# Closing block of a one-core decode kernel: SyncE and ScalarE each await their own store, GpSimd clears its semaphore ranges while the stores fly, SyncE takes the engines' semaphores back

## The chip, the cores and the metric

The kernel runs on one core of a Trainium2 chip (trn2). The time is the device time of one execution, in microseconds. It is longer than the span of the profile, which runs from the start of the first recorded instruction of the kernel to the end of its last one: what the runtime puts ahead of the kernel and behind it has no instruction records in the profile.

## The reference

One token's row `x` (576 values) goes through an attention with a long cache (32 query heads, 16 key and value heads, of 32768 positions the last 4096) and through a dense layer with a gelu, and a gate mixes the two. Everything is bfloat16.

```python
W = min(4096, max(256, Sk // 4))                       # 4096
q = (x @ wq).reshape(B, Sq, Hq, Dh).transpose(0, 2, 1, 3)
k = jnp.repeat(k_cache[:, :, Sk - W:, :], 2, axis=1)   # v the same way
p = softmax(einsum("bhqd,bhkd->bhqk", q, k) * Dh ** -0.5)
a = einsum("bhqk,bhkd->bhqd", p, v).transpose(0, 2, 1, 3).reshape(B, Sq, Hq * Dh) @ wo
b = gelu(x @ w1 + b1) @ w2 + b2
g = sigmoid((x * gate_w).sum(-1, keepdims=True))
out = g * a + (1 - g) * b                              # one row of 576
```

## The kernel before, in words

Nearly all of the work is reading 53.6 MB from HBM: `w1`, `wq`, four loads of the keys, four of the values, `wo` and `w2`, all issued by SyncE's queue in this order, each as soon as its buffer is free. `w2` comes last, in pieces, the last two of 288 and 144 KB. TensorE multiplies each piece as it lands. The last eight columns of `w2` go through `y_late` (line 379), which writes into `y_ps` and `yb_ps`. Then ScalarE turns 192 columns of the result into `out_rows` (line 829) and VectorE the other 96 (line 830), and the two halves of the output row, 576 bytes each, are stored by two DMAs: one issued by ScalarE (line 834), the other by SyncE (line 835).

What follows is the closing block. The program's framework puts a block behind every kernel, in which all engines meet and GpSimd sets the kernel's semaphores back to zero, so that the next execution finds them so. The function `store_ends_program`, called when the program is finalized, replaces that block's list of instructions by a list of its own. In the lines of the profile all of this stands under line 861. These are the words of the function and what they stand for:

- `drain`, `arrive` and `leave` are SyncE's three instructions of the framework's block: the wait for everything, the step that tells the others that SyncE has come, and the wait for the release.
- A *drain* of another engine is an instruction that ends when the engine's work is done.
- S96 is the framework's gather semaphore, which each engine raises by one when it comes; S97 is the release semaphore.
- S99 is GpSimd's own semaphore, S105 VectorE's, S106 ScalarE's, S108 TensorE's; S101 to S104, S107 and S109 are those of loads. S100 is that of SyncE's store (value awaited: 64), S110 that of ScalarE's store (48).
- `lanes` are the semaphores that GpSimd leaves out of its clears because somebody else takes their value back. A taken semaphore is awaited and lowered by the awaited value in one instruction.
- `reset` and `clear` are the pair of instructions by which GpSimd clears a range of semaphores: a drain marked as a reset, and an `EVENT_SEMAPHORE_RANGE_CLEAR`.

The closing block before consists of these instructions, engine by engine:

- SyncE (3): raise S96; await S100 and take it back; await S110 and take it back.
- ScalarE, TensorE, VectorE (1 each): drain, then raise S96.
- GpSimd (10): four instructions that await eight semaphores in pairs (loads, S105, S106); a drain that awaits S99; await S96 at 4 and lower it by 4; then two pairs of reset and clear, for S99 alone and for S101 to S109.

So GpSimd clears only after SyncE, ScalarE, TensorE and VectorE have all come, and SyncE is the engine that waits for the two stores.

Of the kernel before, what the change touches and what calls it, by code (L numbers as in the profile page):

```python
# [18 lines left out]
def kernel(  # L19
# [95 lines left out]
    def store_ends_program(nc):  # L115
        body, end = nc.main_func.blocks[1], nc.main_func.blocks[2]
        sp, pool = mybir.EngineType.SP, mybir.EngineType.Pool
        store = [
            i
            for i in body.instructions  # L120
            if i.engine == sp and type(i).__name__ == "InstDMACopy"
        ][-1]
        act = mybir.EngineType.Activation
        store2 = [
            i
            for i in body.instructions
            if i.engine == act and type(i).__name__ == "InstDMACopy"
        ][-1]
        lanes = sorted(i.sync_info.on_update[0].id for i in (store2, store))
        names = [i.name for i in end.instructions if i.engine == sp]  # L130
        names += [i.name for i in end.instructions if i.engine == act][1:]
        drain, arrive, leave = [i for i in end.instructions if i.engine == sp][:3]
        waits = list(drain.sync_info.on_wait)
        mine = [next(w for w in waits if w.id == lane) for lane in lanes]
        waits = [w for w in waits if w.id not in lanes]
        kept = [
            copy.replace(
                leave,
                name=names.pop(),
                sync_info=mybir.SyncInfo(on_wait=[], on_update=arrive.sync_info.on_update),  # L140
            )
        ]
        for w, name in zip(mine, names):
            taken = mybir.SyncUpdate(
                sync_type="semaphore",
                id=w.id,
                ant_name=w.ant_name,
                update_mode="sem-sub-imm",
                update_value=w.wait_value,
                update_reg=None,  # L150
            )
            kept.append(
                copy.replace(
                    leave,
                    name=name,
                    sync_info=mybir.SyncInfo(on_wait=[w], on_update=[taken]),
                )
            )
        for engine in (
            mybir.EngineType.Activation,  # L160
            mybir.EngineType.PE,
            mybir.EngineType.DVE,
        ):
            kept.append(next(i for i in end.instructions if i.engine == engine))
        ours = [i for i in end.instructions if i.engine == pool]
        others = mybir.SyncInfo(on_wait=waits, on_update=[])
        kept += [copy.replace(ours[0], sync_info=others), ours[1]]
        reset, clear = ours[3:5]
        lo, hi = reset.reset_range_start, reset.reset_range_stop
        edges = [lo - 1, *lanes, hi]  # L170
        spans = [(a + 1, b) for a, b in zip(edges, edges[1:]) if a + 1 < b]
        fresh = [reset.name, clear.name, *[i.name for i in ours[5:7]], *names[len(mine) :]]
        assert len(fresh) >= 2 * len(spans)
        for n, (a, b) in enumerate(spans):
            raw = list(clear.instr)
            assert raw[13:15] == [lo, hi - 1]
            raw[13:15] = [a, b - 1]
            words = dict(clear.ant_dict, range_first=a, range_last=b - 1)
            kept.append(
                copy.replace(reset, name=fresh[2 * n], reset_range_start=a, reset_range_stop=b)  # L180
            )
            kept.append(copy.replace(clear, name=fresh[2 * n + 1], instr=raw, ant_dict=words))
        end.instructions = kept

    nc.at_finalize(store_ends_program)

    const = ctx.enter_context(tc.tile_pool(name="const", bufs=1))
# [34 lines left out]
    for base, pattern, keep in (  # L222
# [6 lines left out]
        n = 1  # L229
# [193 lines left out]
    for c0, src, q in ((0, h_s[0], 2), (1024, h_s[1], 2), (2048, h_m, 4)):  # L423
        n = 1024 if q == 2 else 256
# [92 lines left out]
    issued = {}  # L517
# [348 lines left out]
```

## Time and profile before

| what | value |
|---|---|
| median of 3 runs | 131.51 us (131.38 to 131.53) |
| profiled execution, device time | 131.67 us |
| its span | 130.17 us (130.2 on the page), so 1.50 us lie outside it |
| share of the span in which the chain that ended last waited for DMA | 86% |
| granted TensorE clock, mean | 0.869 |
| HBM read | 53.62 MB, 412 GB/s over the span |

The two profiled numbers belong together: the span holds the kernel's own instructions, closing block included, and the remaining 1.50 us are the runtime's. The trace also records every change of a semaphore, and those go on behind the span, to 131.754 us. The closing block is too short for the page's forty slices (3.25 us each); these are its records, in us from the span's start:

| engine | instruction | start | took, ns |
|---|---|---|---|
| TensorE | drain | 128.149 | 335 |
| VectorE | drain | 128.489 | 283 |
| SyncE | issue of its store | 128.793 | 277 |
| ScalarE | issue of its store | 128.801 | 248 |
| GpSimd | fourth paired wait (S109, S106) | 128.810 | 43 |
| GpSimd | drain, S99 | 128.897 | 41 |
| ScalarE | drain | 129.089 | 240 |
| SyncE | raise S96 | 129.118 | 17 |
| GpSimd | await S96 at 4 | 129.362 | 17 |
| GpSimd | reset, clear of S99 | 129.442, 129.531 | 60, 48 |
| GpSimd | reset, clear of S101 to S109 | 129.608, 129.708 | 70, 88 |
| SyncE | await and take S100 | 130.079 | 17 |
| SyncE | await and take S110 | 130.153 | 17 |

The instructions that wait have the start at which their wait was over. The landing of ScalarE's store is recorded at 129.888, that of SyncE's at 130.063.

### The profile page before, as it was taken

The page shows a single profiled execution, that of the slowest core. Times are in us where ns is not written, and L with a number is a line of the kernel's source. Part 1 is how long each engine was busy: PE and PEld are TensorE (multiplying, and loading weights), DVE is VectorE, ACT ScalarE, POOL GpSimd, SP SyncE. Part 2 cuts the span into 40 slices and gives each one's busy share as a digit, 9 for nine tenths or more (in the row PEclk, how much of TensorE's full clock was granted, in tenths as well). Part 3 has the DMA queues.
Part 4 walks back from the last instruction along what each step waited for, and adds up shares of the span by engine and source line. Part 5 has one row for each costly group of instructions (what it writes and reads, how often), then busy time and mean ns, then how long its engine had stood idle before and what let it go on. Part 6 is the DMA issues. An engine that isn't in the chain of part 4 may idle for free.

```text
span 130.2 us, 1168 instructions
## 1 busy us (share of the span) xinstructions
PE 81.5 (63%) x558; PEld 26.0 (20%) x416; DVE 61.1 (47%) x51; ACT 11.4 (9%) x27; POOL 10.0 (8%) x32
## 2 busy tenths in 40 slices
PE   0003999597106995949949955981075064799994
PEld 0003111310100221201212211331021020426552
DVE  0030003416199659999999995639205005100001
ACT  3032100210300000030003003030000000000000
POOL 7019700010000000000000000000100000000000
PEclk9999999999755799985999999999658757756999
DMA  7999999799899999999999999989989999999970
GB/s 255 398 437 432 476 419 487 342 483 453 383 453 463 398 423 463 433 393 463 433 393 473 423 393 473 453 357 483 435 385 463 451 417 428 417 414 416 398 319 22
DMA packets 2507, 53.70 MB, mean 413 GB/s; under 512 B 287, under 2 KB 420, under 8 KB 710
## 3 DMA queue, kind: packets, MB, share of 16 engines
q1 hardware_dynamic: 2490, 53.61, 96.4%
q8 instruction: 4, 0.07, 0.2%
q10 hardware_dynamic: 12, 0.01, 0.0%
q14 instruction: 1, 0.01, 0.0%
HBM read 53.62 MB, written 0.00 MB: 412 GB/s over the span
## 4 chain that ended last, share of the span: by engine, by line
DMA 86%; DVE 8%; PE 3%; SPq 1%; issue 0%; ACT 0%; DVEq 0%
DMA k_t<-in_A_k_cache_dram 31%; DMA w_t<-in_B_w_dram 29%; DMA v_t<-in_A_v_cache_dram 22%; DVE kt L543 7%; DMA rows<-in_A_x_dram 4%; PE s_ps L654 1%; DVE m L581 1%; PE y_ps L379 1%; SPq L748 0%; SPq L744 0%; SPq L750 0%; PE yb_ps L379 0%; ACT out_rows L829 0%; DVE mr L584 0%; DVEq L543 0%
## 5 line engine op out<-in xcount | busy, mean ns | idle before, releaser
L565 PE MATMUL s_ps<-kt,qz_flat 128*128 128x512 bf16 x128 | 32.5, 410 | 15.4 <-DVE kt L543 8.6
L543 DVE STREAM_TRANSPOSE kt<-k_t 128x4096 f32<-128x4096 f32 x8 | 35.3, 4433 | 5.2 <-DMA k_t<-in_A_k_cache_dram 5.2
L654 PE MATMUL s_ps<-v_t,pt 128*32 128x512 bf16 x96 | 9.1, 547 | 8.9 <-DMA v_t<-in_A_v_cache_dram 8.8
L565 PEld LDWEIGHTS <-qz_flat 128*128 128x128 bf16 x64 | 6.8, 107 | 38.5 <-issue 38.3
L668 DVE TENSOR_TENSOR own<-s_ps,is 128x512 f32<-128x512 f32 x3 | 2.1, 685 | 15.3 <-PE s_ps L654 15.3
L602 ACT ACTIVATE p_t<-s_ps,negm 128x1024 bf16<-128x1024 f32 x4 | 4.5, 1114 | 47.5 <-DVE negm L598 47.5
L400 PE MATMUL s_ps<-w_t,x 128*32 128x512 bf16 x36 | 6.5, 622 | 1.6 <-DVE x L328 1.6
L320 PE MATMUL xs_ps<-ident,rows 1*128 1x1 bf16 x9 | 0.6, 189 | 10.7 <-POOL ident masks.py:199 10.7
L821 DVE COPY y_part<-y_ps 33x96 f32<-33x96 f32 x1 | 0.2, 250 | 14.7 <-PE y_ps L365 14.7
L654 PEld LDWEIGHTS <-pt 128*32 128x32 bf16 x128 | 3.7, 118 | 14.3 <-DMA v_t<-in_A_v_cache_dram 9.2
L425 DVE STREAM_TRANSPOSE turned<-s_ps 128x1024 f32<-128x1024 f32 x2 | 2.5, 1250 | 8.3 <-PE s_ps L400 8.3
L614 DVE STREAM_TRANSPOSE pt<-p_t 128x1024 bf16<-128x1024 bf16 x4 | 4.9, 1225 | 2.7 <-ACT p_t L602 2.7
L365 PE MATMUL y_ps<-wo_t,ov 128*1 128x288 bf16 x62 | 5.7, 359 | 0.3 <-DMA wo_t<-in_A_wo_dram 0.3
L400 PE MATMUL s_ps<-wq_t,x 128*32 128x512 bf16 x36 | 4.9, 620 | 0.9 <-DMA wq_t<-in_A_wq_dram 0.9
L581 DVE TENSOR_REDUCE m<-s_ps 128x1 f32<-128x1024 f32 x4 | 4.8, 1196 | 1.1 <-PE s_ps L565 1.1
L689 PE MATMUL mt_ps<-is,summed 128*128 128x8 f32 x8 | 1.6, 266 | 5.9 <-DVE summed L678 5.9
L705 POOL TENSOR_TENSOR ls<-is,sums 128x32 f32<-128x32 f32 x1 | 0.2, 238 | 60.2 <-ACT p_t L602 60.2
L334 DVE CUSTOM_DVE_ANT_0 rows<-rows 1x576 bf16<-1x576 bf16 x1 | 0.7, 746 | 8.2 <-DMA rows<-in_gate_w_dram 8.2
L678 DVE TENSOR_REDUCE summed<-own 128x128 f32<-128x512 f32 x4 | 4.2, 1041 | 0.1
L365 PEld LDWEIGHTS <-ov 128*1 128x1 bf16 x62 | 3.3, 103 | 3.9 <-issue 1.8
L806 PE MATMUL s_ps<-p_t,ones 128*128 128x512 f32 (+1 forms) x6 | 3.9, 739 | 0.0
L365 PE MATMUL y_ps<-w_t,gt 128*1 128x288 bf16 x56 | 3.8, 286 | 0.0
(87 smaller groups left out, 57.2 us busy)
## 6 DMA issues: line engine op xcount, KB each, us to landing
k_t<-in_A_k_cache_dram SPq DMA_DIRECT2D x4, 4096.0 KB, 33.2
v_t<-in_A_v_cache_dram SPq DMA_DIRECT2D x4, 4096.0 KB, 15.6
wq_t<-in_A_wq_dram SPq DMA_DIRECT2D x1, 4608.0 KB
wo_t<-in_A_wo_dram SPq DMA_DIRECT2D x1, 4464.0 KB, 28.2
w_t<-in_B_w_dram SPq DMA_DIRECT2D x1, 2880.0 KB, 14.3
w_t<-in_B_w_dram SPq DMA_DIRECT2D x1, 2592.0 KB
w_t<-in_B_w_dram SPq DMA_DIRECT2D x1, 2304.0 KB, 8.2
w_t<-in_B_w_dram SPq DMA_DIRECT2D x1, 1440.0 KB
```

Source lines behind the costliest of these rows:

```text
L365: last = nc.tensor.matmul(y_ps[32 * s : 32 * s + wide, :], lhsT=vec, rhs=row[:, DH * s : DH * s + DH], start=start, stop=stop, skip_group_ ...
L400: nc.tensor.matmul(last[n][32 * g : 32 * g + 32], lhsT=vec, rhs=part(n), start=start and g0 == 0, stop=g0 + 4 + g >= len(pieces), skip_gro ...
L425: nc.vector.transpose(out=turned[:, c0 : c0 + n], in_=src[:].rearrange("p (q l j) -> p q j l", q=q, l=32),)
L543: lambda: nc.vector.transpose(out=kt[g, f][:].bitcast(FP32), in_=keys.rearrange("p c d -> p (c d)").bitcast(FP32),),
L565: last = nc.tensor.matmul(s_ps[g][:, u * 512 : (u + 1) * 512].rearrange("p (c k) -> p c k", k=32), lhsT=qz(g, j, 2 * f + half), rhs=kv[:, ...
L581: queue("dve", lambda: nc.vector.reduce_max(out=m1[:], in_=s_ps[g][:], axis=AX.X))
L602: nc.scalar.activation(out=p_t[:].rearrange("p c k -> p (c k)"), in_=s_ps[g][:], func=ACT.Exp, bias=negm[:, 0:1], scale=SCALE, accum_out=s ...
L614: lambda: nc.vector.transpose(out=pt[:, g, :, :].rearrange("p c q -> p (c q)"), in_=p_t[:].rearrange("p c k -> p (c k)"),),
L654: last = nc.tensor.matmul(acc[g][32 * (c % 4) : 32 * (c % 4) + 32, :], lhsT=pt[:, g, c, :], rhs=v_t[g][:, c:NCK:32, :], start=(c < 4), sto ...
L668: lambda: nc.vector.tensor_tensor(out=own[:], in0=acc[g].rearrange("p (c d) -> p c d", c=4), in1=same_c.rearrange("p (c o) -> p c o", o=1) ...
L678: lambda: nc.vector.tensor_reduce(out=summed[g][:], in_=own[:].rearrange("p c d -> p d c"), axis=AX.X, op=ALU.add,),
L806: lambda: nc.tensor.matmul(spare[:, 0:item], lhsT=ones[:], rhs=p_t[:].rearrange("p c k -> p (c k)").bitcast(FP32)[:, 0:item], start=True, ...
```

## The change

The closing block's list is made differently. SyncE no longer raises S96; it awaits S97 (raised by ScalarE's drain, which in exchange no longer raises S96), takes it back, then awaits and takes S105, S106 and S108, and last its own store's S100. ScalarE gets a second instruction behind its drain, which awaits and takes its own store's S110. TensorE's and VectorE's drains raise S96 as before, without the (always fulfilled) wait for S97 at zero. GpSimd awaits the six loads in three pairs and S99 in its drain, no longer S105 and S106; it awaits S96 at 2 in place of 4; and as five semaphores are now left out, it clears four ranges in place of two: S99, S101 to S104, S107, S109.

| engine | instructions in the closing block before | after |
|---|---|---|
| SyncE | 3 | 5 |
| ScalarE | 1 | 2 |
| TensorE, VectorE | 1 each | 1 each |
| GpSimd | 10 | 13 |

```diff
-        lanes = sorted(i.sync_info.on_update[0].id for i in (store2, store))
+        sem, sem2 = (i.sync_info.on_update[0] for i in (store, store2))
...
-        mine = [next(w for w in waits if w.id == lane) for lane in lanes]
-        waits = [w for w in waits if w.id not in lanes]
-        kept = [
+        engines = [n for n in waits if n.startswith(("DVE", "Activation"))]
+        mine = [waits.pop(n) for n in engines]
+        mine.append(
             copy.replace(
-                leave,
-                name=names.pop(),
-                sync_info=mybir.SyncInfo(on_wait=[], on_update=arrive.sync_info.on_update),
+                mine[0],
+                id=pe[0].id,
+                ant_name=pe[0].ant_name,
+                wait_value=sum(u.update_value for u in pe),
             )
-        ]
+        )
+        mine.append(waits.pop(sem.ant_name))
+        last = waits.pop(sem2.ant_name)
+        lanes = sorted(w.id for w in [*mine, last])
+        release = copy.replace(leave.sync_info.on_update[0])
+        issued = copy.replace(release, update_mode="sem-inc")
+        kept = [copy.replace(leave, name=names.pop())]
...
-            kept.append(next(i for i in end.instructions if i.engine == engine))
+            done = next(i for i in end.instructions if i.engine == engine)
+            told = [issued] if engine == act else done.sync_info.on_update
+            kept.append(
+                copy.replace(done, sync_info=mybir.SyncInfo(on_wait=[], on_update=told))
+            )
+        kept.append(
+            copy.replace(
+                [i for i in end.instructions if i.engine == act][1],
+                sync_info=mybir.SyncInfo(
+                    on_wait=[last],
...
         ours = [i for i in end.instructions if i.engine == pool]
-        others = mybir.SyncInfo(on_wait=waits, on_update=[])
-        kept += [copy.replace(ours[0], sync_info=others), ours[1]]
+        others = mybir.SyncInfo(on_wait=list(waits.values()), on_update=[])
+        came = ours[1].sync_info
+        two = mybir.SyncInfo(
+            on_wait=[copy.replace(came.on_wait[0], wait_value=2)],
+            on_update=[copy.replace(came.on_update[0], update_value=2)],
+        )
+        kept += [copy.replace(ours[0], sync_info=others), copy.replace(ours[1], sync_info=two)]
```

## The prediction

> **What bounds the kernel now.** I read the page's chain first, to see whether the closing block is on it.
>
> ```profile
> DMA 86%; DVE 8%; PE 3%; SPq 1%; issue 0%; ACT 0%; DVEq 0%
> ```
>
> The kernel is bound by its loads; nothing in the change touches them, so all it can move lies behind the last of them. The timeline of the end shows where that is.
>
> ```profile
> 128.23 0.21 PE L379 MATMUL yb_ps<-w_t,gt 128*1 128x96 bf16 x2
> 128.44 0.31 ACT L829 CAST out_rows<-y_ps 33x192 bf16<-33x192 f32 x1 [16.13 <-PE yb_ps L379]
> 128.47 0.25 DVE L830 TENSOR_TENSOR out_rows<-yb_ps,y_part 33x96 bf16<-33x96 f32 x1 [1.43 <-PE yb_ps L379]
> 128.79 0.28 SPq L835 DMA_DIRECT2D out_dram<-out_rows  x1
> 128.80 0.25 ACTq L834 DMA_DIRECT2D out_dram<-out_rows  x1
> ```
>
> Both stores are issued at 128.8. Behind them comes line 861, the closing block, asked for by line (columns: engine, instruction, how many, shortest/median/longest in ns, first and last start).
>
> ```profile
> L861 POOLq DRAIN  x3: 41/60/70, 128.9 to 129.6; - x3
> L861 SPq EVENT_SEMAPHORE  x3: 17/17/17, 129.1 to 130.2; - x3
> L861 POOLq EVENT_SEMAPHORE_RANGE_CLEAR  x2: 48/68/88, 129.5 to 129.7; - x2
> L861 ACTq DRAIN  x1: 240/240/240, 129.1 to 129.1; - x1
> ```
>
> By these rows GpSimd is done at 129.8 and SyncE, waiting for the stores, ends the span at 130.170. That suggests that only SyncE counts. The semaphore records behind the span say otherwise. The device time (131.67) reaches 1.50 us past the span, and in that stretch one semaphore of the runtime, S2, steps nine times, at 128.729, 129.483, 130.324, 130.368, 130.392 and then 130.489, 130.528, 130.562, 130.608; some 0.8 us later it steps nine times more with nothing left to wait for: 131.397, .431, .469, .513, .536, .635, .673, .708, .754. It is a chain through the five engines and back, with free hops of 34, 38, 44 and 23 ns, then 99, 38, 35 and 46. Between the two passes some 250 semaphores are set back. In the first pass the hops into the fourth and fifth engine were 44 and 24 ns, the free ones: those two were ready already, and **whoever is third came last**.
>
> Who is third? The first step (128.729) can only be TensorE's: no other engine was through. The second (129.483) follows ScalarE's drain (129.089 + 0.240 = 129.329) by 0.154. For the rest I compare with the release at the program's start: S97 is raised at 0.705 and lowered by SyncE 34 ns later, by ScalarE after 45, by VectorE after 58; GpSimd answers the gather (0.578) after 49. Less 11 to 14 ns, these are the free hops: 23 (fifth, SyncE), 34 (second, ScalarE), 38 (third, GpSimd), 44 (fourth, VectorE). So I take the third to be **GpSimd**, whose last clear ended at 129.708 + 0.088 = 129.796, and which stepped 0.528 later. SyncE, done at 130.170, was ready before its turn at 130.368.
>
> **The change part by part.**
>
> *GpSimd's start.* Before, its wait for S96 at 4 ended at 129.362, after ScalarE's drain (its raise at 129.338). After, S96 needs TensorE (raised 128.498) and VectorE (128.783); with the same 24 ns it ends at 128.807. The paired waits ahead of it are over by then: the last load's semaphore came at 128.106, and S105 and S106 are no longer awaited here. Moved ahead: 129.362 − 128.807 = 0.555.
>
> *GpSimd's clears.* From the wait to the first reset 80 ns; the pair for S99 takes 166 ns to the next reset; a later pair has 100 ns from reset to clear, and its clear 48 ns for one semaphore or 88 for nine, thus an estimated 63 for four, with some 29 ns to the next instruction. Four pairs: 166 + (100 + 63 + 29) + (100 + 48 + 29) + (100 + 48) = 683. GpSimd ends at 128.807 + 0.080 + 0.683 = 129.570, 0.226 sooner than now. If the unseen 0.528 stays, it steps at 130.098 (bounds for that piece: 0.154 as ScalarE has, which puts it at 129.72, and 0.528).
>
> *SyncE.* Its raise of S96 goes. Its wait for S97 ends some 16 ns after ScalarE's drain, at about 129.35; four instructions lie in its queue ahead of the store's wait, 74 ns each (130.079 to 130.153): 129.65 at the latest. The store lands at 130.063, so 0.41 us hide them; without that cover they would cost up to 0.30. The semaphores that it takes (VectorE, ScalarE, TensorE) had been final since 128.76. Its wait ends at 130.079, and the instruction at 130.096: the second store's wait, 74 ns, has left it. When is it ready for the chain? Bounds: the 0.154 of ScalarE, and at most 130.368 − 130.170 = 0.198, since it held up nothing; below, zero. I take 0.154, the row of the most similar engine: 130.250.
>
> *ScalarE.* It now awaits its store behind the drain: landing 129.888, then 16 + 17 ns, 129.921; with its 0.154 it steps at 130.075 (129.483 before, where it held nobody). Behind it come the hops of GpSimd, VectorE and SyncE: 130.075 + 0.038 + 0.044 + 0.024 = 130.181. Nothing of the kernel is queued behind this wait; only the chain's later engines wait for it.
>
> *The sum.* SyncE's turn in the chain is the latest of three: its own 130.250; GpSimd's 130.098 + 0.044 + 0.024 = 130.166; ScalarE's 130.181. That is 130.250 against 130.392, **0.142 us sooner**, and the rest follows unchanged: 131.67 − 0.142 = 131.53 for the profiled execution, which lies 0.16 above the median; from the median, 131.51 − 0.142 = 131.37. What is late next is SyncE's store. Bounds: with SyncE's piece at 0.198 the gain is 0.098; with both stores landing at the earlier time, 129.888, ScalarE's path decides and it is 0.211; with the later landing, 130.063, on ScalarE's store, its path gives 130.063 + 0.033 + 0.154 + 0.106 = 130.356 and the gain is 0.036. So 0.04 to 0.21, that is 131.30 to 131.47, before the scatter of the medians (0.15 us over three runs). A measurement of this kernel can tell some 0.2%, 0.26 us, from no change: the whole bracket lies inside.
>
> **The rivals.**
>
> *Only the second wait counts.* If the third in the chain were SyncE, its step would be 130.170 + 0.154 = 130.324, exactly the one recorded, and GpSimd's move would be worth nothing. The gain is then the 74 ns of the removed instruction: 131.44. For it speaks that coincidence; against it, that hops of 44 and 24 ns would then belong to GpSimd and VectorE in an order that the rows of the start don't show. The same price follows wherever a store's landing decided already before the change: the issue at 128.793 and the landing at 130.063 are 1.27 us apart, and had it been 0.05 us more, SyncE (ready 0.154 behind its end, at 130.324) would have been last in either kernel. Chance 0.13. The Trainium skill ("DMA: Bandwidth & Descriptors", Anatomy of one DMA — SWDGE (gpsimd) path) puts a DMA's fixed cost at about 2.0 us, fitted to DMAs that GpSimd issues, and names the write's receipt as most of it; by that the landing would come at an estimated 130.79, and this rival would hold. The trace's 1.27 us speak against that figure here.
>
> *The stores land sooner.* Behind the store's last packets (129.557 and 129.589) the landings follow after 0.331 and 0.474 us, and GpSimd's second clear, 129.708 to 129.796, falls between. If the clears hold up the landings, moving them ahead brings both to about 129.76 (0.17 to 0.20 behind their packets, below any row here: the four small loads of the start needed 0.34 to 0.51). SyncE would be ready at 129.76 + 0.033 + 0.154 = 129.95, ScalarE's path at 130.05, and GpSimd's 130.166 would decide, unless its unseen piece shrinks too; with both, 130.05: a gain of 0.34, 131.17. Against it: it needs two things, and the landings after short packets take as long elsewhere. Chance 0.2.
>
> *A fetch of instructions comes behind the last store (slower).* The trace has one packet of instructions of 8 KB near the end, from 129.968 to 130.310, 14 ns ahead of the chain's third step.
>
> ```profile
> q14 instruction: 1, 0.01, 0.0%
> ```
>
> It may be what GpSimd's 0.528 consists of: 0.172 until the packet starts, 0.342 for it, 0.014. The closing block gets longer on SyncE (2 instructions), ScalarE (1) and GpSimd (3). The point from which this decides is a block's edge: if SyncE's code, or ScalarE's, now crosses one behind its store's wait, that piece follows the landing: 130.096 + 0.528 = 130.624 in place of 130.392, a loss of 0.23; with the engine's own 0.154 besides, 0.39, so 131.74 to 131.90. Against it: one packet only is seen, although all five engines run the same kind of end, and SyncE's stream is among the shortest. The Trainium skill ("Runtime: NRT & Kernel Launch", Instruction fetch mechanics) holds that crossing a block is mostly hidden, while a taken branch out of the resident window stalls; by the first there is no loss, and the trace does not show whose packet it is. Chance 0.12.
>
> *The change doesn't do what it says:* SyncE ends when its store lands, in either kernel, and if the profiled landing was late by chance GpSimd's gain is real, if early, nothing is gained. That is the lower end of my bracket and not counted apart.
>
> **How the numbers follow.** The forecast, 131.37, has 0.55; the second wait alone 0.13; the sooner landing 0.2; the fetch 0.12. The first two lie within 0.2% but for scatter that might carry the forecast past it (0.05). So faster by over 0.2%: 0.2 + 0.05 = 0.25; slower 0.12; within 0.2%: 0.63. The range reaches from 131.19, most of the way to the sooner landing, to 131.60, the bracket's upper end and the scatter, and leaves the fetch out. The likeliest case's own range is 131.25 to 131.52.
>
> **What would show it right or wrong.** In the changed profile: GpSimd's wait for S96 ends near 128.81 and its last of four clears near 129.57; SyncE's last instruction starts some 16 ns after its store's landing and none follows; ScalarE's second instruction likewise; the gap from the last instruction to the chain's fifth step is near 0.154 in place of 0.222 (130.392 − 130.170). I am wrong if the third step still comes 0.5 us behind the landings, if the time moves by more than 0.26 us, or if the 8 KB packet stands behind SyncE's end.

## The result and the profile after

The changed kernel takes 131.23 us in the median of 22 runs (131.06 to 132.05), the kernel before 131.53 (131.38 to 132.86) beside it. The ratio is 0.9975, interval 0.9964 to 0.9986: 0.33 us faster (0.18 to 0.47). Two later measurements of the same kernel gave 0.9978 (0.9965 to 0.9990) and 0.9983 (0.9974 to 0.9993), that is 0.29 and 0.22 us. The profiled execution took 131.21 us with a span of 129.94.

The page's chain shows nothing of it. Its first row is the same, to the digit, as before:

```profile
DMA 86%; DVE 8%; PE 3%; SPq 1%; issue 0%; ACT 0%; DVEq 0%
```

The timeline of the end (start, duration, engine, line) ends with the same rows, all some 0.16 us earlier in the span; in nine profiles of the two kernels and of variants with two stores, the stores' issue lies anywhere from 128.54 to 128.79, so that is taken for scatter of the loads.

```profile
128.28 0.31 ACT L869 CAST out_rows<-y_ps 33x192 bf16<-33x192 f32 x1 [16.20 <-PE yb_ps L419]
128.31 0.25 DVE L870 TENSOR_TENSOR out_rows<-yb_ps,y_part 33x96 bf16<-33x96 f32 x1 [1.50 <-PE yb_ps L419]
128.63 0.28 SPq L875 DMA_DIRECT2D out_dram<-out_rows  x1
128.64 0.25 ACTq L874 DMA_DIRECT2D out_dram<-out_rows  x1
```

The closing block, now line 901 (engine, instruction, how many, shortest/median/longest ns, first and last start):

```profile
L901 POOLq DRAIN  x5: 41/54/69, 128.1 to 129.2; - x5
L901 SPq EVENT_SEMAPHORE  x5: 17/17/17, 129.2 to 129.9; - x5
L901 POOLq EVENT_SEMAPHORE  x4: 17/43/43, 126.9 to 128.6; - x4
L901 POOLq EVENT_SEMAPHORE_RANGE_CLEAR  x4: 44/46/48, 128.8 to 129.3; - x4
L901 ACTq DRAIN  x1: 251/251/251, 128.9 to 128.9; - x1
L901 ACTq EVENT_SEMAPHORE  x1: 17/17/17, 129.8 to 129.8; - x1
```

What to see: the four clears start at 128.8 and are over at 129.3, where the two of before started at 129.5 and ended at 129.8. GpSimd's last wait now ends at 128.6, as the stores are issued. SyncE's last instruction starts at 129.9, ScalarE's at 129.8; nothing follows either.

The rest is in the trace's records of the runtime's semaphore S2, behind the span. To compare executions, all times in this table and below count from the issue of SyncE's store.

| us behind the issue of SyncE's store | before | after |
|---|---|---|
| GpSimd's wait for the gather ends | 0.569 | 0.014 |
| GpSimd's last clear ends | 1.003 | 0.708 |
| ScalarE's store lands | 1.095 | 1.098 |
| SyncE's store lands | 1.270 | 1.272 |
| SyncE's last instruction ends | 1.377 | 1.305 |
| chain, step 2 (ScalarE) | 0.690 | 1.274 |
| step 3 (GpSimd) | 1.531 | 1.313 |
| step 4 (VectorE) | 1.575 | 1.357 |
| step 5 (SyncE) | 1.599 | 1.438 |
| step 6 (first of the way back) | 1.696 | 1.482 |
| last step of the second pass | 2.961 | 2.746 |

Step 6 comes 0.214 us sooner, and from there to the last step it is 1.265 and 1.264 us: what the closing block wins by step 6 is kept to the end.

The names of the engines in the table are readings. In the kernel before step 1 comes 0.064 us ahead of the store's issue and VectorE's drain ends 0.021 ahead of it, later, so step 1 is TensorE's; the experiments delay ScalarE, GpSimd and SyncE one by one and so show steps 2, 3 and 5. That leaves step 4 for VectorE; no run delayed VectorE itself.

### The profile page after: what moved, and what is told of

The parts are those of the page before. It is cut to its first block, busy times and chain, and to the rows that moved or that the text cites. A ratio compares the mean times of both kernels' runs of the same rounds, so it can differ in the third digit from the quotient of the medians.

```text
span 129.9 us, 1174 instructions
## 1 busy us (share of the span) xinstructions
PE 81.6 (63%) x558; PEld 25.9 (20%) x416; DVE 61.1 (47%) x51; ACT 11.4 (9%) x27; POOL 10.0 (8%) x32
## 4 chain that ended last, share of the span: by engine, by line
DMA 86%; DVE 8%; PE 3%; SPq 1%; issue 0%; ACT 0%; DVEq 0%
DMA k_t<-in_A_k_cache_dram 31%; DMA w_t<-in_B_w_dram 29%; DMA v_t<-in_A_v_cache_dram 22%; DVE kt L583 7%; DMA rows<-in_A_x_dram 4%; PE s_ps L694 1%; DVE m L621 1%; PE y_ps L419 1%; SPq L788 0%; SPq L784 0%; SPq L790 0%; PE yb_ps L419 0%; ACT out_rows L869 0%; DVE mr L624 0%; DVEq L583 0%
```

## The experiments

All are the kernel before or the changed one with an edit in `store_ends_program`, the two with one store also in the store itself. Each was timed against the kernel before on the same chip, in five rounds.

**Both stores awaited by SyncE.** The changed kernel without ScalarE's wait:

```diff
...
-        last = waits.pop(sem2.ant_name)
-        lanes = sorted(w.id for w in [*mine, last])
+        mine.append(waits.pop(sem2.ant_name))
+        lanes = sorted(w.id for w in mine)
...
-        kept.append(
-            copy.replace(
-                [i for i in end.instructions if i.engine == act][1],
...
```

> The changed kernel, but SyncE awaits both stores again, its own (S100) first and ScalarE's (S110) behind it; GpSimd still clears early. Counted from the issue of SyncE's store, the runtime's chain took its sixth step at 1.696 us before and at 1.482 after. If GpSimd's late clears were what held the chain: SyncE ends one wait (74 ns) later than in the changed kernel, 1.379 us behind the issue, its step follows 0.133 later and the sixth step 0.044 behind that, 1.556; so 0.14 us faster than before, 0.07 slower than the changed kernel. If only SyncE's second wait counted: back at 1.70, no gain over before. If the clears held up the landings: S100 lands 1.27 us behind the issue as in both kernels, and that says nothing for it.

Measured: ratio 0.9982 (0.9969 to 0.9996), 131.22 against 131.49. In the profile:

```profile
L883 SPq EVENT_SEMAPHORE  x6: 17/17/17, 129.3 to 130.1; - x6
L883 POOLq EVENT_SEMAPHORE_RANGE_CLEAR  x4: 44/46/48, 128.9 to 129.4; - x4
```

Step 2 is back at 0.692, since ScalarE awaits nothing. GpSimd's last clear ends at 0.716 and its step comes at 1.250, 0.534 later; SyncE ends at 1.372, steps at 1.510, and step 6 is at 1.554, 2 ns from what was expected. So the early clears alone bring 0.142 us of the trace's 0.214, with both waits where they were.

**The same, in the other order.** Against the run just shown:

```diff
-        mine.append(waits.pop(sem.ant_name))
         mine.append(waits.pop(sem2.ant_name))
+        mine.append(waits.pop(sem.ant_name))
```

> As the first, but SyncE awaits ScalarE's store (S110) first and its own (S100) second. S110 landed 0.174 us sooner in both profiles, so its wait is over while S100 still flies. If GpSimd held the chain before, splitting the waits over two engines is worth nothing and the order alone matters: sixth step at 1.48, as the changed kernel, 0.21 faster than before. If ScalarE's own wait is what the gain comes from: 1.70 and no gain.

Measured: ratio 0.9986 (0.9972 to 1.0000), 131.26. Step 6 at 1.486, the changed kernel's 1.482 within 4 ns. SyncE's wait for S110 is over while S100 still flies, and its last instruction ends at 1.305, as in the changed kernel. So what the second wait costs at SyncE's end, 67 ns here (1.372 against 1.305), can be had by order alone; by the trace it is not needed that each engine awaits its own store. The times, 131.22 and 131.26, cannot tell 0.07 us.

**Only the split.** The kernel before, with ScalarE's wait as in the change and everything else as it was:

```diff
-        mine = [next(w for w in waits if w.id == lane) for lane in lanes]
+        mine = [next(w for w in waits if w.id == store.sync_info.on_update[0].id)]
+        last = next(w for w in waits if w.id == store2.sync_info.on_update[0].id)
...
+        kept.append(
+            copy.replace(
+                [i for i in end.instructions if i.engine == act][1],
+                sync_info=mybir.SyncInfo(
+                    on_wait=[last],
...
```

> The kernel before, but ScalarE awaits its own store behind its drain and SyncE only its own; the gather at 4, two ranges, late clears as before. If GpSimd held the chain: third step still 0.528 behind the last clear, sixth at 1.70, no change (within 0.03). If SyncE's second wait counted: 0.07 faster, sixth at 1.62.

Measured: ratio 1.0004 (0.9991 to 1.0017), 131.45.

```profile
L880 SPq EVENT_SEMAPHORE  x2: 17/17/17, 129.0 to 130.0; - x2
L880 POOLq EVENT_SEMAPHORE_RANGE_CLEAR  x2: 48/68/88, 129.4 to 129.6; - x2
L880 ACTq EVENT_SEMAPHORE  x1: 17/17/17, 129.8 to 129.8; - x1
```

The span did get shorter at its end (SyncE's last instruction ends at 1.306, not 1.377), and in the trace it is worth nothing: GpSimd's clears end at 1.005, it steps at 1.533, and step 6 is at 1.698. The interval alone would allow 0.07 us as well. But the time outside the span grew: the executions' time less their span (on record in tenths) is 1.49 us in the mean, 1.44 for the kernel before in the same rounds.

**Late clears in the changed kernel.** One instruction of SyncE more, behind its wait for ScalarE's drain, raises S96, and GpSimd waits for 3:

```diff
-        kept = [copy.replace(leave, name=names.pop())]
+        kept = [
+            copy.replace(leave, name=names.pop()),
+            copy.replace(
+                leave,
+                name="I-2000000",
+                sync_info=mybir.SyncInfo(on_wait=[], on_update=arrive.sync_info.on_update),
+            ),
+        ]
...
-            on_wait=[copy.replace(came.on_wait[0], wait_value=2)],
-            on_update=[copy.replace(came.on_update[0], update_value=2)],
+            on_wait=[copy.replace(came.on_wait[0], wait_value=3)],
+            on_update=[copy.replace(came.on_update[0], update_value=3)],
```

> The changed kernel, but GpSimd awaits S96 at 3, the third raise being one more instruction of SyncE behind its wait for ScalarE's drain: the clears start late again, and there are four of them. If GpSimd steps 0.528 us behind its last clear, as the prediction read the profile of before: its wait ends some 0.69 behind the issue of SyncE's store, the clears 0.69 later, 1.39; third step 1.92, sixth 2.08, 0.39 us slower than before and 0.6 slower than the changed kernel. If that 0.528 was no property of GpSimd (the third step being SyncE's): no change against the changed kernel, 0.2 to 0.3 faster than before. If the tail is as short as ScalarE's 0.154: third step 1.54, sixth 1.71, about as before.

Measured: 1.0024 (1.0013 to 1.0034), 131.72 us: 0.32 us slower than before (0.17 to 0.45). In its profile the closing block by line, with the columns as above:

```profile
L908 SPq EVENT_SEMAPHORE  x6: 17/17/17, 129.1 to 129.8; - x6
L908 POOLq EVENT_SEMAPHORE_RANGE_CLEAR  x4: 44/46/48, 129.4 to 129.9; - x4
L908 ACTq EVENT_SEMAPHORE  x1: 17/17/17, 129.7 to 129.7; - x1
```

The clears run from 129.4 to 129.9, with SyncE and ScalarE through their waits at 129.8 and 129.7, 6 ns later behind the store's issue than in the changed kernel, and the span (129.93) is as short as the changed kernel's. Yet the time is the longest of the two-store kernels. GpSimd's last clear ends at 1.385, its step comes at 1.920, step 6 at 2.085; 1.92 and 2.08 had been expected. This is the run that decides. That its profile's span is 0.24 us shorter than the kernel before's is scatter, since the store is issued at 128.54 here and at 128.79 there; behind the issue the last instruction ends at 1.385 here and at 1.377 there, nearly the same. Yet the kernel is 0.32 us slower, and what grew lies outside the span: 1.84 us in the mean of the executions, 1.44 before. GpSimd's end does not count where it is recorded but 0.53 us later.

**The changed kernel again, and one store in place of two.**

> The changed kernel once more, beside the two single-store kernels. Sixth step 1.48 us behind the issue of SyncE's store, S110's landing at 1.10, S100's at 1.27, 0.2 to 0.3 us faster than before. ScalarE's path (landing, then the hops of GpSimd and VectorE, then VectorE's 0.12 until its next step) gives 1.480, SyncE's (landing, 0.033, 0.133, one hop of 0.044) 1.482: both decide at once.

Measured: 0.9978 (0.9965 to 0.9990), 131.21 us; step 6 at 1.478, landings at 1.094 and 1.268.

```diff
-    nc.scalar.dma_start(out=halves[1:2, :], in_=out_rows[32:33, :])
-    nc.sync.dma_start(out=halves[0:1, :], in_=out_rows[0:1, :])
+    nc.sync.dma_start(out=halves, in_=out_rows[0:33:32, :])
```

> The changed kernel with one store of both rows (2 x 288) issued by SyncE in place of two of one row each; SyncE awaits it, ScalarE awaits nothing, GpSimd clears early and three ranges. If the later landing of S100 (1.27 against 1.10) comes from standing second behind the other store: the one store lands at about 1.10, SyncE steps at 1.27 and the sixth step is at 1.31, 0.17 us sooner than in the changed kernel, 0.38 than before. If it comes from the queue of SyncE itself: landing 1.27, sixth step 1.48, as the changed kernel. GpSimd would step at 1.08 and hold nothing.

Measured: 1.0014 (0.9999 to 1.0029), 131.55 us: both expectations missed. The timeline shows why:

```profile
128.44 0.60 SPq L855 DMA_DIRECT2D out_dram<-out_rows  x1
```

Issuing two rows in one DMA takes 0.60 us in place of 0.28. The first packet leaves 0.63 us behind the issue's end, where SyncE's store had 0.49 after the change, so 0.33 of the delay is the issue and some 0.13 stays open. The last packet starts at 1.276, and the landing, 0.341 behind it, is at 1.617. SyncE steps at 1.783 and step 6 is at 1.827, 0.13 later than before; the measured loss is 0.18 (-0.01 to 0.38). Beside the changed kernel of the same rounds (131.21, step 6 at 1.478) step 6 is 0.35 later and the time 0.34 longer. GpSimd, three clears, ends at 0.583 and steps at 1.118.

The same store from ScalarE (`nc.scalar.dma_start`):

> The same single store, issued and awaited by ScalarE. If the landing is at 1.10 in either queue, ScalarE steps at 1.28 and the chain's hops through GpSimd and VectorE and VectorE's 0.12 follow: sixth step 1.48, as the changed kernel and 0.17 later than with SyncE, since the early place in the chain costs what the landing saves. If the place in the chain doesn't matter: 1.31, as with SyncE.

Measured: 1.0017 (1.0006 to 1.0028), 131.71 us: the landing expected at 1.10 and both times for step 6 are missed, as with SyncE.

```profile
128.61 0.56 ACTq L873 DMA_DIRECT2D out_dram<-out_rows  x1
```

The landing came at 1.59 behind the issue's start; from the landing to step 6 it takes 0.387 us, where it took 0.210 with SyncE. That difference was what the pair was to show: a wait that ends last costs 0.18 more on ScalarE, second in the chain, than on SyncE, fifth. The two medians lie 0.16 us apart.

**The two kernels once more, for the size.**

> The kernel before against itself: ratio 1 within its interval, and a second profile of it. If the trace's 0.21 us is the whole gain of the change, its chain takes the third step 0.53 behind the last clear and the sixth 1.70 behind the issue of SyncE's store again, and the issue itself lies anywhere in the 128.5 to 128.8 that the profiles so far show for either kernel. If some 0.1 us of the measured 0.3 comes from ahead of the stores, the issue is at 128.75 or later again.

Measured: ratio 0.9996 (0.9972 to 1.0020); last clear at 1.003, third step at 1.532, sixth at 1.697, and the store's issue at 128.68, so not late as a rule.

> The changed kernel a third time, beside the kernel before against itself on the same chip. 0.21 us faster if the closing block is the whole of it, 0.30 if the two measured medians so far are right to the hundredth; the sixth step at 1.48 behind the store's issue, the issue between 128.5 and 128.8.

Measured: 0.9983 (0.9974 to 0.9993), 131.17 us: 0.22 us faster (0.09 to 0.34). Step 6 at 1.501, with SyncE's store landing at 1.291 in this execution; the issue at 128.59.

Over all the runs the move of step 6 against the kernel before reaches from 0.218 us sooner to 0.389 later, and in each it lies inside the interval of the measured change (counted from ScalarE's store where SyncE has none).

## Why the prediction was right, and where its size was off

- *What bounds the end.* Right. That the third step was GpSimd's and held the chain, not SyncE's, was read from hops of 23 to 44 ns; late clears and the split alone show it on the chip. With the split SyncE ends 71 ns sooner and the third step stays (1.533 against 1.531); that SyncE's end with its 0.154 gave the recorded step too was coincidence. The unseen piece behind GpSimd's last clear stayed: 0.528 and 0.529 in the two profiles of before, 0.534 or 0.535 with three or four clears wherever GpSimd's own turn was the late one. What it consists of stays open. (Between the chain's two passes the trace has 196 changes of semaphores, not the prediction's some 250; nothing rests on that.)
- *GpSimd's start.* 128.807 was predicted, 0.014 behind the store's issue; measured 0.014.
- *GpSimd's clears.* 0.763 us was predicted from the wait to the end of the fourth clear, measured 0.694: the resets took 49 to 69 ns, and the clear of four semaphores 47, not 63. It decided nothing, since GpSimd was ready (0.708 + 0.534 = 1.242) before ScalarE's step at 1.274.
- *ScalarE.* Its step was predicted 1.282 behind the issue, measured 1.274. The cost of its wait was named: through its hops, the path that gave 0.211.
- *SyncE.* Its end was predicted at 1.303, measured 1.305; its own piece at 0.154, measured 0.133.
- *The sum: the term that was mis-sized.* "SyncE's turn in the chain is the latest of three" set the gain at 0.142. The trace gives 0.214, just past the 0.211 of my upper bound. Of the missing 0.072, 0.019 is SyncE's turn itself: the fifth step moved by 0.161 (1.599 to 1.438), since SyncE's own piece was shorter than my 0.154. The other 0.053 lies behind it. I took a late fifth step to delay the rest by as much. But VectorE needs some 0.12 us between its own step and its answer to SyncE's (1.575 to 1.696 before), and these cover SyncE's lateness: after, SyncE stepped 81 ns behind VectorE and the answer came 125 ns behind it. The free hops that I had written down, 23 and then 99, hold this number. By VectorE's 0.122 of the second pass (23 and 99), ScalarE's path ends at 1.357 + 0.122 = 1.479, and SyncE's at 1.438 + 0.044 = 1.482: the two decide within 3 ns of each other. So the term mis-sized is what SyncE's turn costs, by 0.07 us. The remainder of the measured 0.33, some 0.1 us, is not in the trace of the closing block, and all three intervals hold 0.214. The two repeats bound it: outside the span the mean fell from 1.45 and 1.44 to 1.32 and 1.28 us, where the trace has 0.143 between the last instruction and the last step (1.584 to 1.441). The mean span fell by 0.11 and 0.13, where the trace has 0.072; the 0.04 to 0.06 left over are no more than the scatter of these means. So there is no clear sign of a gain outside the closing block.
- *The chances.* The first two ratios lie just past the 0.2% line that I had drawn and the last one inside it, so "within 0.2%" was no safe answer: a trace's 0.21 us is 0.16%, and I had put it at 0.11%.
- *Luck.* 131.23 lies in the stated range, but below the 131.25 to 131.52 of the case that I held for likeliest; the range reached there only for the sooner landing, which did not happen. By the time alone that rival (131.17) fits better than the forecast (131.37); only the trace tells them apart. A move of more than 0.26 us was also named as a sign of being wrong, and the first two measurements, 0.33 and 0.29, show one. Their intervals reach down to 0.18 and 0.13, and the closing block moved as forecast, so I take it for scatter and too small a sum, not for another mechanism.
- *The rivals.* Only the second wait counts: refuted by step 6 of the split alone. The stores land sooner: 1.095 and 1.270 before, 1.098 and 1.272 after, with the clears moved 0.3 us ahead of them; refuted. The fetch behind the last store: the 8 KB packet starts at 1.175 in one profile of before and at 1.432 in the other, with the chain the same to 2 ns, so it holds none of these steps. In the changed kernel it starts at 1.413, behind SyncE's end, which I had named as a sign of being wrong, and at 1.153 and 1.159 in that kernel's other two profiles; that sign was badly chosen.

The Trainium skill ("Runtime: NRT & Kernel Launch", The ~15µs preamble/postamble breakdown) gives a barrier across the five engines as eight hops of 44 ns, some 355 ns in all, for the one ahead of the kernel, and names another behind it that waits for all engines. The trace agrees for the one behind: the pass with nothing to wait for took 357 ns over eight hops, of 23 to 47 ns but for VectorE's 97 to 99 on the way back. The entry of a late engine costs more here, 0.13 to 0.14 us for SyncE, 0.14 to 0.16 for ScalarE and 0.53 for GpSimd. The Trainium skill ("DMA: Bandwidth & Descriptors", Anatomy of one DMA — SWDGE (gpsimd) path) gives some 2.0 us as a DMA's fixed cost, fitted to DMAs that GpSimd issues. The trace does not bear it out for these: the 576-byte stores here, from SyncE and ScalarE, took 1.09 to 1.29 us from issue to semaphore.

## What to carry to other kernels

The end of the span is not the end of the time: look for what the runtime waits for behind it, and put each engine's last instruction, with that engine's own delay added, into that order. Here a kernel whose last instruction ended 8 ns later was 0.32 us slower, and an end 71 ns sooner was worth nothing by the trace. Work that has to be done by the engine with the longest delay, GpSimd, belongs ahead of waits that other engines can take; and when two waits sit on one engine, first await what lands first.

## What was not expected of the hardware

- Of two 576-byte stores issued within 8 to 13 ns of each other, SyncE's landed 0.17 to 0.19 us behind ScalarE's in all nine two-store profiles, though its last packet left only 0.032 us later: 0.475 against 0.333 from packet to semaphore after the change. In the one store of two rows both increments came within 4 ns, 0.341 behind the last packet from SyncE and 0.338 from ScalarE, so it is not SyncE's queue as such. Whether two stores on one DMA engine follow one another so was not tried.
- One DMA of two rows of 576 bytes takes 0.56 to 0.60 us to issue, one of a single row 0.25 to 0.28.
